# One queue of loads that the planner spaces by transfer time, layer norm of blocks 4 to 7 turned on TensorE, and all Q and K casts on ScalarE

## The chip, the cores and the metric

The kernel runs on 1 core of one Trainium2 chip. The metric is the device time of one execution in microseconds (us). A core has five instruction streams that run side by side and meet through semaphores: PE (TensorE, matmuls and their weight loads PEld), DVE (VectorE), ACT (ScalarE), POOL (GpSimd) and SP (SyncE), which here issues all DMAs but one. Each stream executes its instructions in program order, so an instruction that waits holds up everything behind it on its engine. This holds for SP as well.

## What is computed

A transformer block with modulation on x of 2048 tokens by 448 channels, in bfloat16. Cut to what matters:

```
sa, ca, ga, sb, cb, gb = split(silu(c) @ w_mod, 6)
h   = layernorm(x) * (1 + ca) + sa                       # LN1
q, k, v = split(h @ wqkv)                                # 16 heads of 28
o   = softmax over 8 keys at distances 0, 2, .. 14 (q k) v
x   = x + ga * (o @ wo)
h   = layernorm(x) * (1 + cb) + sb
y   = layernorm(h)                                       # LN of the MLP
x   = x + gb * (gelu(y @ w1 + b1) @ w2 + b2)             # hidden size 1792
```

## The kernel before

The tokens are 16 blocks of 128 (`NBLK`), even tokens in blocks 0 to 7 and odd ones in 8 to 15, so that the dilation of 2 becomes plain neighbourhood. The front of a block (`front_ln`, `front_qk`) is LN1 on token rows, a turn to channel rows (`hT`), and the products Q, K (`pq`) and V (`pv`). Blocks 0 and 1, then 2 and 3, then 4 to 7, 8 to 11 and 12 to 15 go together; we call the last three chunks 1, 2 and 3. V is written to memory (`v_hbm`, L712) and read back in windows (`vb`, L772), one pair of loads for each of nine attention steps b = 0 to 8 of 228 queries. An attention step is `lt` (logits, PE), Exp on ACT, a mask on DVE (`et`), `pd` and `po` on PE (denominator and output), Ln and Exp on ACT, and a product on DVE (`oT`). Then come `pw` (output projection), LN2 and the LN of the MLP on DVE, a DMA transpose to `yT` (L893), and for every 512 tokens the MLP: `p` at L578 and L584 (w1), gelu on ACT (L927), and `p` at L938 (w2).

How LN1 is turned is decided in `front_ln` by `early`. Chunk 0 (blocks 0 to 3) is turned on PE (`ptr`, L632), and ACT and DVE scale the result out of PSUM (L645, L641). The others are turned by DMA transposes on SP (L650, four for a chunk), after which DVE scales them in SBUF (L654). The row scale comes from two small ACT instructions for chunk 0 and from POOL for the others. `front_qk` lets eight casts of a chunk leave PSUM, and `QKE` says which by ACT (L694, A) and which by DVE (L691, D).

The order of every engine's work is made by a planner when the program is built (`Planner`): each piece of work is a task with an engine, a cost in us, and `late`, the time from its end until its result can be used. The planner plays the engines forward by priority and emits the tasks in the order in which it started them, so its costs set the order. For loads, `load` counts an issue of 0.5 us and keeps a running estimate of when the queue will be free; all its loads are chained by `order_after`, in the order in which they are written. `bulk` does the same for the MLP's weights, chained behind the load of `mod_bc` (the modulation rows for all partitions, L734).

Of the kernel before, what the change touches and what calls it, by code (L numbers as in the profile page):

```python
# [12 lines left out]
BF16 = mybir.dt.bfloat16  # L13
# [64 lines left out]
class Planner:  # L78
# [6 lines left out]
    def add(self, eng, us, fn, reads=(), writes=(), bufs=(), after=(), order_after=(), rank_add=0.0, late=0.0, dense=1.0, port=False, mode="F"):  # L85
        t = Task(len(self.tasks), eng, us, fn, bufs, rank_add, late, dense, port or eng == "POOL", mode)
# [191 lines left out]
def kernel(  # L278
# [14 lines left out]
    nc = tc.nc  # L293
# [6 lines left out]
    add = P.add  # L300
# [6 lines left out]
    def ps_one(shape, name, dtype=FP32):  # L307
        return Buf("S", lambda k: ps.tile(shape, dtype, name=name, tag=f"S{k}"), name)
# [18 lines left out]
    gbb2_bc = cst.tile([128, D], FP32, name="gbb2_bc")  # L327
    b1_bf = cst.tile([128, FT], BF16, name="b1_bf")
    b1_col = cst.tile([128, FT], FP32, name="b1_col")
# [36 lines left out]

    dma = {"free": 0.0, "at": 0.0, "last": []}

    def load(fn, nbytes, writes, reads=(), bufs=()):
        issue = 0.5  # L370
        dma["at"] += issue
        start = max(dma["free"], dma["at"] + 0.6)
        dma["free"] = start + nbytes / 360e3
        t = add("SP", issue, fn, writes=writes, reads=reads, bufs=bufs, late=dma["free"] + 1.0 - dma["at"],
                order_after=dma["last"])
        dma["last"] = [t]
        return t

    def load_k(dst, src, key, bufs=()):
        n = src.shape[1]  # L380
        for h in range(2):
            load(lambda h=h: nc.sync.dma_start(out=dst()[:, 2 * h:2 * h + 2],
                                               in_=src[KOFF[2 * h]:KOFF[2 * h] + 256].rearrange("(kt p) n -> p kt n", p=128)),
                 256 * n * 2, [key + "ab"[h]], bufs=bufs)

    def load_x(b0, b1):
        load(lambda: nc.sync.dma_start(out=x_all[:, b0:b1, :], in_=xv[b0 // 8, :, b0 % 8:(b1 - 1) % 8 + 1, :]),
             (b1 - b0) * 128 * D * 2, [f"x{b}" for b in range(b0, b1)])

    def bulk(fn, nbytes, writes, bufs=()):  # L390
        us = nbytes / 300e3
        t = add("SP", us, fn, writes=writes, bufs=bufs, late=2.5, order_after=dma["last"])
        dma["last"] = [t]

# [30 lines left out]
    def load_mlp():
        bulk(lambda: nc.sync.dma_start(out=b2_bc.t[:], in_=B_b2.partition_broadcast(128)), 128 * D * 2, ["b2"], [b2_bc])
        bulk(lambda: nc.sync.dma_start(out=b1_bf[:], in_=B_b1.rearrange("(f p) -> p f", p=128)), 150e3, ["b1_bf"])
        for kt in range(KT):
            bulk(lambda kt=kt: nc.sync.dma_start(out=w1_s[:, kt], in_=B_w1[KOFF[kt]:KOFF[kt] + 128]), F * 256, [f"w1{kt}"])
        for i in range(4):  # L430
            f0, f1 = 4 * i, min(4 * i + 4, FT)
            bulk(lambda f0=f0, f1=f1: nc.sync.dma_start(
                out=w2_s[:, f0:f1], in_=B_w2[128 * f0:128 * f1].rearrange("(ft p) n -> p ft n", p=128)),
                (f1 - f0) * 256 * D, [f"w2l{f // 2}" for f in range(f0, f1, 2)])
        add("DVE", 0.1, lambda: nc.vector.tensor_copy(out=b1_col[:], in_=b1_bf[:]), reads=["b1_bf"], writes=["b1"])

# [234 lines left out]
    def front_qk(bs, engs):  # L671
# [24 lines left out]
        for b in bs[::2]:  # L696
# [10 lines left out]
            for i in range(2):  # L707
# [9 lines left out]
    def mods():  # L717
# [3 lines left out]
        def mm():  # L721
# [243 lines left out]
    for pi, (blocks, tiles) in enumerate(PHASES):  # L965
        exps.clear()
        lt_mms.clear()
        for b in blocks:
            attention(b, tbl, prev_w1)
            if b in FRONTS:  # L970
                fc = FRONTS.index(b) + 1
                bs = list(range(4 * fc, 4 * fc + 4))
                front_ln(bs)
                front_qk(bs, QKE[1])
                if fc == 1:
                    mods()
                if fc == 2:
# [43 lines left out]
```

## Time and profile before

| | us |
|---|---|
| median of 3 runs | 188.71 (188.1 to 189.67) |
| the profiled execution | 188.94 |
| its span in the trace | 187.2 |
| busy in the span: PE, DVE, ACT, POOL | 166.3, 119.9, 103.4, 46.8 |

In the rows below, busy times are sums over an engine's instructions, "idle before" is the time that the engine stood before a group with what released it in brackets, and SPq rows are DMA issues (their length is the time until SP goes on, not that of the transfer). PEclk is the granted TensorE clock as a share of full speed: 1.00 is 2.4 GHz and 0.50 is 1.2 GHz. A matmul row's start is exact, its end is modelled.

### The profile page before, as it was taken

Reading aid. Unit: us, or ns where it says so; the run is one execution under the profiler, and the core shown is the slowest. Engines: PE = TensorE matmul, PEld = TensorE weight load, DVE = VectorE, ACT = ScalarE, POOL = GpSimd, SP = SyncE. Lnnn points to the kernel's source line nnn. Section 1 sums busy time; section 2 is a strip of 40 time slices with the busy share of each in tenths; the row PEclk is TensorE's granted clock in tenths of the full one; section 3 lists DMA queues with packets and bytes.
Section 4 is the critical chain, followed back from the end, with each engine's and each line's share of the span. In section 5 each row is a group of like instructions: output and inputs, shape, how many; then the busy total and the mean of one; then the engine's idle time right before and its main releaser. Section 6 shows DMA issues by size and latency. Waiting matters only on the chain.

```text
span 187.2 us, 4950 instructions
## 1 busy us (share of the span) xinstructions
PE 166.3 (89%) x2039; PEld 77.1 (41%) x2053; DVE 119.9 (64%) x329; ACT 103.4 (55%) x181; POOL 46.8 (25%) x81
## 2 busy tenths in 40 slices
PE   7799903699999799999999999999899999999992
PEld 2455402134444343433455434455433445333550
DVE  2798360894999999899844507998769982001121
ACT  3249626058548875947867883756863720365200
POOL 4062000150073433024422002458132353000000
PEclk9999965589999999999999999999999999999999
DMA  5999834499577893430151310005500025000011
GB/s 166 360 380 289 230 84 104 147 200 209 126 199 255 261 225 112 82 122 0 39 76 53 88 28 0 4 1 157 62 2 0 4 56 154 0 0 27 26 49 49
DMA packets 32649, 20.71 MB, mean 111 GB/s; under 512 B 18069, under 2 KB 31986, under 8 KB 32626
## 3 DMA queue, kind: packets, MB, share of 16 engines
q1 hardware_dynamic: 32624, 20.39, 41.0%
q8 instruction: 16, 0.26, 0.6%
q14 instruction: 7, 0.06, 0.1%
q10 hardware_dynamic: 2, 0.00, 0.0%
HBM read 12.75 MB, written 3.96 MB: 89 GB/s over the span
## 4 chain that ended last, share of the span: by engine, by line
PE 68%; DMA 16%; DVE 7%; SPq 3%; issue 2%; ACT 2%; DVEq 0%
PE p L938 21%; PE p L578 20%; PE pq L578 10%; DMA x_all<-in_A_x_dram 6%; PE p L584 4%; PE pw L867 4%; DMA yT<-y 3%; DMA wmod<-in_w_mod_dram 3%; DMA wqk_st<-in_A_wqkv_dram 3%; PE pv L578 3%; PE pq L584 2%; DVE st_all L501 2%; DVE et L804 2%; SPq L650 2%; PE po L826 1%
## 5 line engine op out<-in xcount | busy, mean ns | idle before, releaser
L927 ACT ACTIVATE hm<-p,b_col 128x512 bf16<-128x512 f32 x56 | 35.2, 686 | 29.2 <-PE p L584 13.4
L938 PE MATMUL p<-w_s,hm 128*128 128x448 bf16 x224 | 44.9, 353 | 0.0
L578 PE MATMUL p<-yT,w_s 128*128 128x512 bf16 x160 | 38.2, 380 | 2.1 <-DMA yT<-y 1.2
L519 POOL TENSOR_TENSOR rs_all<-tv_all,neg_half 128x1 f32<-128x1 f32 (+1 forms) x35 | 23.3, 677 | 56.4 <-DVE tv_all L516 51.5
L578 PE MATMUL pq<-hT,Wqk 128*128 128x512 bf16 (+1 forms) x115 | 25.3, 350 | 5.5 <-DVE hT L654 4.5
L938 PEld LDWEIGHTS <-hm 128*128 128x128 bf16 x224 | 20.9, 98 | 19.7 <-issue 0.9
L897 POOL TENSOR_TENSOR x1p<-x_all,gbb_bc 128x448 f32<-128x448 bf16 x16 | 17.0, 1072 | 46.2 <-DVE x_all L871 37.8
L945 DVE TENSOR_TENSOR x_all<-p,x1p 128x448 bf16<-128x448 f32 x16 | 9.8, 619 | 29.0 <-PE p L938 28.9
L796 ACT ACTIVATE et<-lt 128x464 bf16<-128x464 f32 x36 | 17.3, 565 | 13.9 <-PE lt L786 13.9
L578 PEld LDWEIGHTS <-w_s 128*128 128x128 bf16 x168 | 15.2, 98 | 22.7 <-issue 6.8
L501 DVE BATCH_NORM_STATS2 st_all<-x_all 128x6 f32<-128x448 bf16 x32 | 18.8, 611 | 3.8 <-DMA x_all<-in_A_x_dram 3.7
L578 PEld LDWEIGHTS <-Wqk 128*128 128x128 bf16 x120 | 10.5, 100 | 16.7 <-issue 5.8
L524 DVE TENSOR_SCALAR z<-x_all,mv,rs_all 128x512 bf16<-128x512 bf16 (+1 forms) x32 | 12.8, 417 | 3.9 <-DMA hT<-z 2.3
L871 DVE TENSOR_TENSOR x_all<-pw,x_all 128x448 bf16<-128x448 f32 x16 | 9.6, 618 | 8.2 <-PE pw L867 8.2
L804 DVE TENSOR_TENSOR et<-et,mask 128x928 bf16<-128x928 bf16 x18 | 12.5, 727 | 3.3 <-ACT et L796 3.3
L867 PE MATMUL pw<-wo_s,oT 128*128 128x448 bf16 x64 | 13.8, 354 | 0.7 <-DVE oT L852 0.7
L852 DVE TENSOR_TENSOR oT<-po,den 128x456 bf16<-128x456 f32 x18 | 10.6, 623 | 2.9 <-ACT den L842 2.9
L694 ACT CAST kT<-pq 128x512 bf16<-128x512 f32 (+1 forms) x15 | 7.3, 505 | 7.7 <-PE pq L584 5.6
L826 PE MATMUL po<-et,vb 64*32 64x57 bf16 x576 | 6.7, 195 | 5.2 <-DMA vb<-v_hbm 5.2
L708 ACT CAST vstage<-pv 128x448 bf16<-128x448 f32 x16 | 7.9, 540 | 5.2 <-PE pv L584 4.4
L578 PE MATMUL pv<-Wv,hT 128*128 128x448 bf16 x48 | 10.5, 354 | 0.0
L694 ACT CAST qT<-pq 128x512 bf16<-128x512 f32 (+1 forms) x15 | 7.1, 502 | 5.8 <-PE pq L584 3.7
(81 smaller groups left out, 169.5 us busy)
## 6 DMA issues: line engine op xcount, KB each, us to landing
w_s<-in_B_w_dram SPq DMA_DIRECT2D x7, 448.0 KB
vb<-v_hbm SPq DMA_DIRECT2D x18, 128.0 KB, 2.7
v_hbm<-vstage SPq DMA_DIRECT2D x8, 256.0 KB, 2.6
wmod<-in_w_mod_dram SPq DMA_DIRECT2D x4, 448.0 KB, 7.2
out_dram<-x_all SPq DMA_DIRECT2D x8, 224.0 KB, 2.3
wqk_st<-in_A_wqkv_dram SPq DMA_DIRECT2D x4, 226.0 KB, 5.2
wm_st<-in_w_mod_dram SPq DMA_DIRECT2D x2, 448.0 KB
x_all<-in_A_x_dram SPq DMA_DIRECT2D x1, 896.0 KB, 10.4
```

What stands on the lines that cost most here:

```text
L501: add("DVE", 0.53, lambda: nc.vector.bn_stats(out=st_all[:, sl, :], in_=src()), reads=key, writes=[f"st{sl}"])
L519: lambda: nc.gpsimd.tensor_tensor(out=rs_all[:, which, b0:b0 + n], in0=tv_all[:, which, b0:b0 + n], in1=neg_half[:, 0:n], op=ALU.pow),
L524: return add("DVE", us, lambda: nc.vector.tensor_scalar(out=dst(), in0=src(), scalar1=mv[:, b, 0:1], scalar2=rs_all[:, which, b:b + 1], op ...
L578: nc.tensor.matmul(outs[i].t[:], lhsT=w(i, kt, slice(0, 128)), rhs=x(i, kt, slice(0, 128)), start=(n == 0 and not last), stop=(n == 2 and ...
L584: nc.tensor.matmul(outs[i].t[:], lhsT=w(i, kt, rows), rhs=x(i, kt, rows), start=not last, stop=last, tile_position=(r0, 0))
L694: add("ACT", 0.06 + n / 1200, lambda dst=dst, p=pq[i]: nc.scalar.copy(out=dst, in_=p.t[:]), bufs=[pq[i]], writes=w)
L796: ex = add("ACT", 0.45, lambda r=r: nc.scalar.activation(out=et.t[:, r].rearrange("p n ft c -> p (n ft c)"), in_=lts[r].t[:].rearrange("p ...
L804: nc.vector.tensor_tensor(out=ev, in0=ev, in1=mask[:], op=ALU.mult)
L867: nc.tensor.matmul(pw.t[:], lhsT=oT[:, ft, c0:c0 + 128], rhs=wo_s[:, ft, :], start=(ft == 0), stop=(ft == 3))
L897: P.wrote(add("POOL", 1.05, lambda: nc.gpsimd.tensor_tensor(out=xp.t[:], in0=x_all[:, t, :], in1=gbb2_bc[:], op=ALU.add), reads=[f"x{t}", ...
L927: gl = add("ACT", 0.57, lambda f=f, p=p1[i]: nc.scalar.activation(out=hm_at(f), in_=p.t[:], func=ACT.Gelu_apprx_tanh, bias=b1_col[:, f:f + ...
L938: nc.tensor.matmul(p2.t[:], lhsT=hm_at(f)[:, bi * 128:(bi + 1) * 128], rhs=w2_s[:, f, :], start=(f == 0), stop=(f == FT - 1))
```

## The change

It does six things. Every load gets a planner cost of its bytes divided by `DMA_RATE` (330 GB/s, at least 0.5 us) on SP and a `late` of 1.8. Only the first loads, to x of blocks 4 to 7, stay chained; the others are `free` and the planner places each where its priority puts it. The load of x of blocks 8 to 15 becomes two of 448 KB. Chunk 1 becomes `early`. All Q and K casts go to ACT. And b1 arrives as 14 rows and is turned by one small matmul (`b1_cols`).

```diff
-QKE = ("ADAAADAA", "ADAAADAA")
+QKE = ("AAAAAAAA", "AAAAAAAA")
...
+DMA_RATE = 330e3
...
-    def load(fn, nbytes, writes, reads=(), bufs=()):
-        issue = 0.5
-        dma["at"] += issue
-        start = max(dma["free"], dma["at"] + 0.6)
-        dma["free"] = start + nbytes / 360e3
-        t = add("SP", issue, fn, writes=writes, reads=reads, bufs=bufs, late=dma["free"] + 1.0 - dma["at"],
-                order_after=dma["last"])
-        dma["last"] = [t]
-        return t
+    chain_dma = []
+
+    def load(fn, nbytes, writes, reads=(), bufs=(), free=False):
+        t = add("SP", max(0.5, nbytes / DMA_RATE), fn, writes=writes, reads=reads, bufs=bufs, late=1.8,
+                order_after=list(chain_dma))
+        if not free:
+            chain_dma[:] = [t]
...
-    load_x(8, 16)
+    for b in (8, 12):
+        load_x(b, b + 4)
...
-        early = ch == 0
+        early = ch <= 1
...
-            add("SP", 0.5, lambda r0=r0, vs=vs: nc.sync.dma_start(
+            add("SP", 0.8, lambda r0=r0, vs=vs: nc.sync.dma_start(
                 out=v_hbm[r0:r0 + 256].rearrange("(b p) n -> p b n", p=128), in_=vs.t[:].rearrange("p b h d -> p b (h d)")),
...
-        add("SP", 0.5, lambda: nc.sync.dma_start(out=mod_bc[:], in_=mod_hbm[:].rearrange("i n -> (i n)").partition_broadcast(128)),
+        add("SP", 1.4, lambda: nc.sync.dma_start(out=mod_bc[:], in_=mod_hbm[:].rearrange("i n -> (i n)").partition_broadcast(128)),
             reads=["mod_hbm"], writes=["ga", "sb", "g2", "gb"], late=3.2)
-        dma["last"] = [P.tasks[-1]]
-        load_mlp()
...
+    def b1_cols():
+        pb1 = ps_one([128, FT], "pb1")
+        P.wrote(add("PE", 0.1, lambda: nc.tensor.matmul(pb1.t[:], lhsT=b1_rows[:], rhs=ident[0:FT, 0:FT], start=True, stop=True),
+                    mode="32x128", reads=["b1_rows", "ident"], bufs=[pb1]), pb1)
+        add("DVE", 0.1, lambda: nc.vector.tensor_copy(out=b1_col[:], in_=pb1.t[:]), bufs=[pb1], writes=["b1"])
```

The MLP's loads, before in `load_mlp`, stand behind the two loads of x as `free` loads; the wmod loads (`w_mod`, for the later modulation rows), the four of wo and `v_pads` are `free` too.

The first place is SP, before, from the loads of the later modulation weights (two tiles, two halves each) to the DMA transposes of chunk 1. wo is the output projection, `vstage_105` and `vstage_106` hold V of two blocks each.

```order
L382 DMA wmod_214<-in_w_mod_dram 128x2x896 x2
L420 DMA wo_s<-in_A_wo_dram 28x4x448 x4
L387 DMA x_all<-in_A_x_dram 128x8x448
L712 DMA v_hbm<-vstage_105 128x2x512
L772 DMA vb<-v_hbm 64x2x512 x2
L650 DMA_TRANSPOSE hT<-z 128x4x128 x4
L712 DMA v_hbm<-vstage_106 128x2x512
L732 DMA mod_hbm<-mod_rows 4x448
```

The same place with the change. The line numbers are those of the changed file: 379, 384 and 412 are the loads, 702 and 766 the V store and the `vb` load, 722 and 724 the modulation rows, 640 the DMA transposes, which here are those of chunk 2.

```order
L379 DMA wmod_253<-in_w_mod_dram 128x2x896
L702 DMA v_hbm<-vstage_105 128x2x512
L384 DMA x_all<-in_A_x_dram 128x4x448
L412 DMA wo_s<-in_A_wo_dram 28x4x448 x2
L766 DMA vb<-v_hbm 64x2x512 x2
L384 DMA x_all<-in_A_x_dram 128x4x448
L722 DMA mod_hbm<-mod_rows 4x448
L412 DMA wo_s<-in_A_wo_dram 28x4x448
L702 DMA v_hbm<-vstage_106 128x2x512
L412 DMA wo_s<-in_A_wo_dram 28x4x448
L420 DMA w_s<-in_B_w_dram 128x1792
L724 DMA mod_bc<-mod_hbm 128x1792
L640 DMA_TRANSPOSE hT<-z 128x4x128 x4
```

The V store of blocks 0 and 1 moved ahead of wo and of x of blocks 8 to 15, and the `vb` pair that waits for it ahead of x of 12 to 15. No transpose stands between them any more, and the transposes of chunk 2 stand behind `mod_bc` and a w1 piece.

The second place is DVE from the scaling of blocks 2 and 3 on, before.

```order
L641 TENSOR_SCALAR hT<-ptr,mod_col 128x256 x2
L524 TENSOR_SCALAR z<-x_all,mv_100,rs_all 128x512 x4
L804 TENSOR_TENSOR et<-et,mask 128x928 x2
L691 CAST kT<-pq 128x256
L691 CAST qT<-pq 128x256
L501 BN_STATS st_all<-x_all 128x6 x3
```

And with the change, where 631 is the scaling out of PSUM, 514 the normalization, 798 the mask and 491 the statistics.

```order
L631 TENSOR_SCALAR hT<-ptr,mod_col 128x256 x2
L514 TENSOR_SCALAR z<-x_all,mv_100,rs_all 128x512 x4
L798 TENSOR_TENSOR et<-et,mask 128x928 x2
L631 TENSOR_SCALAR hT<-ptr,mod_col 128x512 x2
L491 BN_STATS st_all<-x_all 128x6 x2
```

The two casts are gone and the scaling of chunk 1 stands in their place, ahead of the statistics of blocks 8 to 11. Before, chunk 1 was scaled behind those statistics.

On PE, between the modulation rows (`pb`) and `pd` of attention step 0 there was nothing before. With the change two pairs of `pq` of blocks 2 and 3, `pv` of blocks 4 and 5 and one pair of `pq` of chunk 1 stand there, and the sixteen PE transposes of chunk 1 stand just ahead of `pb`.

The third place is SP with the change, ahead of the first MLP tile: 887 is the transpose to `yT` (four of these make the first tile) and the vb load stands between the third and the fourth.

```order
L887 DMA_TRANSPOSE yT<-y 128x4x128
L766 DMA vb<-v_hbm 64x2x512 x3
L887 DMA_TRANSPOSE yT<-y 128x4x128
L766 DMA vb<-v_hbm 64x2x512
L887 DMA_TRANSPOSE yT<-y 128x4x128
L702 DMA v_hbm<-vstage_106 128x2x512
```

Before, the second to fourth of these four transposes stood together, ahead of a pair of `vb` loads.

## Rows read from the trace of the kernel before

**Rows 1.** Windows by stage: busy us of each engine, clock, DMA share, GB/s.

```profile
core 0: us, PE busy (x) PEld busy (x) DVE busy (x) ACT busy (x) POOL busy (x), PEclk, DMA share, GB/s
0.00:22.70 22.70, 19.85 (x232) 10.70 (x235) 14.44 (x49) 11.79 (x30) 6.46 (x30) 1.00 0.95 293
22.70:34.30 11.60, 1.85 (x144) 1.39 (x140) 4.46 (x14) 4.38 (x8) 0.00 (x0) 0.60 0.39 96
34.30:48.50 14.20, 13.91 (x186) 5.48 (x188) 10.57 (x28) 7.53 (x13) 3.23 (x3) 0.84 0.86 190
48.50:80.50 32.00, 29.30 (x470) 13.21 (x473) 30.83 (x83) 23.36 (x42) 10.43 (x14) 1.00 0.65 176
80.50:187.20 106.70, 101.37 (x1016) 46.36 (x1024) 59.64 (x160) 56.30 (x88) 26.71 (x34) 1.00 0.18 43
28.30:38.60 10.30, 5.53 (x139) 2.42 (x141) 4.96 (x16) 3.44 (x6) 1.02 (x1) 0.50 0.54 143
```

**Rows 2.** Timeline of PE around its two longest waits: start, us, operation.

```profile
28.32 0.73 PE L826 MATMUL po<-et,vb 64*32 64x57 bf16 x64 [5.23 <-DMA vb<-v_hbm]
...
34.31 0.61 PE L578 MATMUL pq<-hT,Wqk 128*128 128x512 bf16 x1 [4.53 <-DVE hT L654]
```

**Rows 3.** Timeline of SP's DMA issues in the same stretch.

```profile
7.85 2.31 SPq L382 DMA_DIRECT2D wmod<-in_w_mod_dram  x4
...
13.62 0.39 SPq L387 DMA_DIRECT2D x_all<-in_A_x_dram  x1
14.88 2.03 SPq L712 DMA_DIRECT2D v_hbm<-vstage  x1
24.75 1.33 SPq L772 DMA_DIRECT2D vb<-v_hbm  x2
26.17 5.22 SPq L650 DMA_TRANSPOSE hT<-z  x4
```

**Rows 4.** Pieces of the chain of work that ended last: start, us, what.

```profile
13.62 10.44 DMA x_all<-in_A_x_dram
...
30.18 2.44 DMA hT<-z
```

**Rows 5.** DMA issues of the page: KB each, us to landing.

```profile
vb<-v_hbm SPq DMA_DIRECT2D x18, 128.0 KB, 2.7
v_hbm<-vstage SPq DMA_DIRECT2D x8, 256.0 KB, 2.6
wmod<-in_w_mod_dram SPq DMA_DIRECT2D x4, 448.0 KB, 7.2
```

**Rows 6.** Timeline of DVE: normalization of chunk 1, its scaling.

```profile
16.70 1.37 DVE L524 TENSOR_SCALAR z<-x_all,mv,rs_all 128x512 bf16<-128x512 bf16 x4
...
32.74 1.52 DVE L654 TENSOR_SCALAR hT<-hT,mod_col 128x512 bf16<-128x512 bf16 x4 [5.72 <-DMA hT<-z]
```

**Rows 7.** Timeline of PE: the transposes of chunk 0.

```profile
7.33 0.61 PE L632 MATMUL ptr<-ident,z 128*128 128x128 bf16 x8
...
15.12 0.90 PE L632 MATMUL ptr<-ident,z 128*128 128x128 bf16 x8
```

**Rows 8.** By line: durations in ns, least, median and most.

```profile
L691 DVE CAST qT<-pq x5: 392/681/692, 11.0 to 72.8; 128x512 bf16<-128x512 f32 x3, 128x256 bf16<-128x256 f32 x2
L694 ACT CAST qT<-pq x15: 372/586/592, 10.7 to 75.4; 128x512 bf16<-128x512 f32 x9, 128x256 bf16<-128x256 f32 x6
L645 ACT ACTIVATE hT<-ptr,mod_col x4: 553/561/566, 8.5 to 16.3; 128x256 bf16<-128x256 bf16 x4
L632 PE MATMUL ptr<-ident,z x16: 216/219/230, 7.3 to 15.8; 128*128 128x128 bf16 x16
```

**Rows 9.** Timeline of PE where the first MLP tile begins.

```profile
77.60 1.31 PE L578 MATMUL pv<-Wv,hT 128*128 128x448 bf16 x6
79.24 0.93 PE L867 MATMUL pw<-wo_s,oT 128*128 128x448 bf16 x4 [0.33 <-DVE oT L852]
80.51 1.46 PE L578 MATMUL p<-yT,w_s 128*128 128x512 bf16 x5 [0.34 <-DMA yT<-y]
```

More of the change, by code (lines that the diff above doesn't have):

```diff
@@ L85, in add @@
     def add(self, eng, us, fn, reads=(), writes=(), bufs=(), after=(), order_after=(), rank_add=0.0, late=0.0, dense=1.0, port=False, mode="F"):
-        t = Task(len(self.tasks), eng, us, fn, bufs, rank_add, late, dense, port or eng == "POOL", mode)
+        t = Task(len(self.tasks), eng, us, fn, bufs, rank_add, late, dense, (port or eng == "POOL") and port is not None, mode)
         for k in list(reads) + [b for b in bufs]:
@@ L327 @@
     gbb2_bc = cst.tile([128, D], FP32, name="gbb2_bc")
-    b1_bf = cst.tile([128, FT], BF16, name="b1_bf")
+    b1_rows = cst.tile([FT, 128], BF16, name="b1_rows")
     b1_col = cst.tile([128, FT], FP32, name="b1_col")
@@ L365, in wide, with load_k @@
         return bass.AP(ap.tensor, ap.offset, [ap.ap[0], [KOFF[2], 2], [1, 256]])
-    dma = {"free": 0.0, "at": 0.0, "last": []}
-    def load(fn, nbytes, writes, reads=(), bufs=()):
-        issue = 0.5
-        dma["at"] += issue
-        start = max(dma["free"], dma["at"] + 0.6)
-        dma["free"] = start + nbytes / 360e3
-        t = add("SP", issue, fn, writes=writes, reads=reads, bufs=bufs, late=dma["free"] + 1.0 - dma["at"],
-                order_after=dma["last"])
-        dma["last"] = [t]
-        return t
-    def load_k(dst, src, key, bufs=()):
+    chain_dma = []
[4 more added lines that the diff above has]
+            chain_dma[:] = [t]
+    def load_k(dst, src, key, bufs=(), free=False):
         n = src.shape[1]
@@ L383, in load_k @@
                                                in_=src[KOFF[2 * h]:KOFF[2 * h] + 256].rearrange("(kt p) n -> p kt n", p=128)),
-                 256 * n * 2, [key + "ab"[h]], bufs=bufs)
+                 256 * n * 2, [key + "ab"[h]], bufs=bufs, free=free)
     def load_x(b0, b1):
         load(lambda: nc.sync.dma_start(out=x_all[:, b0:b1, :], in_=xv[b0 // 8, :, b0 % 8:(b1 - 1) % 8 + 1, :]),
[L388 to L393, printed above, removed]
+             (b1 - b0) * 128 * D * 2, [f"x{b}" for b in range(b0, b1)], free=b0 >= 8)
     add("DVE", 0.2, lambda: nc.vector.memset(warm_w[:], 0.0), writes=["warm_w"], rank_add=500)
@@ L412, in v_pads @@
                           in_=z.unsqueeze(1).to_broadcast([LEAD, 3, DP]))
-    load(v_pads, 3 * LEAD * DP * 2, ["v_pads"], reads=["warm_w"])
+    load(v_pads, 3 * LEAD * DP * 2, ["v_pads"], reads=["warm_w"], free=True)
     for i in range(2):
-        load_k(lambda i=i: wmod2[i].t[:], w_mod[:, (2 + 2 * i) * D:(4 + 2 * i) * D], f"wmod2{i}", [wmod2[i]])
+        load_k(lambda i=i: wmod2[i].t[:], w_mod[:, (2 + 2 * i) * D:(4 + 2 * i) * D], f"wmod2{i}", [wmod2[i]], free=True)
     add("POOL", 1.6, lambda: nc.gpsimd.memset(wo_s[:], 0.0), writes=["wo"], rank_add=440)
@@ L420 @@
         load(lambda r=r: nc.sync.dma_start(out=wo_s[HP * r:HP * r + DH, :, :], in_=wo_v[r]), D * D // 2, [f"wo{r}"],
-             reads=["wo"])
-    load_x(8, 16)
+             reads=["wo"], free=True)
+    for b in (8, 12):
+        load_x(b, b + 4)
     b2_bc = sb("zh", [128, D], BF16, "b2_bc")
[L425 to L435, printed above, removed]
+    load(lambda: nc.sync.dma_start(out=b2_bc.t[:], in_=B_b2.partition_broadcast(128)), 128 * D * 2, ["b2"], bufs=[b2_bc], free=True)
+    load(lambda: nc.sync.dma_start(out=b1_rows[:], in_=B_b1.rearrange("(f p) -> f p", p=128)), F * 2, ["b1_rows"], free=True)
+    for kt in range(KT):
+        load(lambda kt=kt: nc.sync.dma_start(out=w1_s[:, kt], in_=B_w1[KOFF[kt]:KOFF[kt] + 128]), F * 256, [f"w1{kt}"], free=True)
+    for i in range(4):
+        f0, f1 = 4 * i, min(4 * i + 4, FT)
+        load(lambda f0=f0, f1=f1: nc.sync.dma_start(
+            out=w2_s[:, f0:f1], in_=B_w2[128 * f0:128 * f1].rearrange("(ft p) n -> p ft n", p=128)),
+            (f1 - f0) * 256 * D, [f"w2l{f // 2}" for f in range(f0, f1, 2)], free=True)
     def pool(us, fn, writes, reads=(), rank_add=300, gated=True):
@@ L976 @@
                     mods()
+                    b1_cols()
                 if fc == 2:
```

## The prediction

> **What bounds the kernel now.** I began with the busy time by stage [rows 1]. From 80.5 us to the end PE is busy for 101.37 of 106.70 us at full clock. The change puts no new instruction there, so I let that stretch pass unchanged: a start that is earlier by some amount ends earlier by the same amount. From 48.5 to 80.5 PE is busy for 29.30 of 32.00 us and DVE for 30.83, so DVE is nearly full and PE stands still for 2.70. The odd stretch is 22.70 to 34.30: PE is busy for 1.85 of 11.60, and neither DVE (4.46) nor ACT (4.38) fills it. Nothing computes, so something is on its way.
>
> The timeline of PE names two waits [rows 2]: 5.23 us for the `vb` load of attention step 0 and 4.53 us for the scaled `hT` of chunk 1. The clock adds to them: after PE has stood still, the rows from 28.30 to 38.60 show a granted clock of 0.50 (1.2 GHz), with 5.53 us of PE busy in them [rows 1].
>
> Why both come late is seen on SP [rows 3, 4]. The load of x of blocks 8 to 15, 896 KB, is issued at 13.62 and has landed 10.44 later, at 24.06. The V store of blocks 0 and 1 is issued at 14.88, behind it on the same queue. The `vb` pair must wait for that store and is issued at 24.75. The four transposes of chunk 1 stand behind the pair: they begin at 26.17 and take SP 5.22 us, the last lands 2.44 after 30.18, and DVE scales for 1.52 more. Yet the token rows of chunk 1 were normalized by 16.70 + 1.37 = 18.07 [rows 6].
>
> **LN1 of chunk 1 on PE.** It takes four DMA transposes off SP. Instead PE gets sixteen. The trace has eight in 0.61 and eight in 0.90 us [rows 7], so sixteen cost 1.2 to 1.8; I take 1.5, since the second row has a gap that may come again. Each is 219 ns long when looked at alone [rows 8], so 3.5 would be the price if none overlapped. The b1 matmul is smaller than one of them; I give it 0.1. The Trainium skill speaks against this step: TensorE: Matmul & The Clock Gate, "Part 4: PE-mode transpose", gives about 275 ns for a 128x128 transpose inside a kernel; an estimate by that figure is 4.4 us for sixteen, and the time would be 2.9 later than mine. This trace does not agree, since eight of them began and ended within 0.61 us.
>
> Scaling out of PSUM: DVE has two instructions of 512 columns, which I price as its cast of 512 out of PSUM, 0.69 at most, so 1.4 against the 1.52 that go [rows 6, 8]: nothing. ACT has two new ones of 512. At 256 one takes 561 ns [rows 8], so a lies between 0.56 and 1.12; an ACT cast grows from 372 to 586 from 256 to 512, so I take 0.8, 1.6 for both, off the path unless ACT fills.
>
> When is chunk 1 ready? Its rows end at 18.07 now. Its row scale moves to ACT, behind the scaling of blocks 2 and 3, and costs about 1.5, so 19.6. PE turns it until 21.1, DVE and ACT scale it until about 22.5 to 23. Now it is ready at 34.26. PE meanwhile has `pb` and two pairs of blocks 2 and 3 to do, so it finds chunk 1 ready. Its one wait is for the normalized rows ahead of the transposes: 0 to 1.5, I take 0.6.
>
> **The order of the loads.** With the change only the wmod loads stand ahead of the V store: the last is issued at about 9.8, and with the median of 7.2 us to landing [rows 3, 5] it is in at 17. The store is issued about 15.3 (its casts stand behind two more ACT casts), and lands 2.6 later when alone: 17.9 at the earliest, 2.6 after wmod, 19.6, if it queues behind it, and 24.75 at the latest, as now; I take 19.5. The `vb` pair takes SP 1.33, and 644 KB of x and wo are ahead of it on the queue, 2.2 us at the 293 GB/s of the first stage [rows 1]. That puts `vb` at about 24 instead of 28.32. PE comes to it at about 27.5, because two pairs, one `pv` and one pair of chunk 1 stand ahead of it now. So this wait goes, and with `vb` at the old time it would be 0.8.
>
> So 9.75 us of standing still (11.60 - 1.85) have work to put in. If PE does not stand still the half clock goes too: 5.53 us of work at half speed are 2.77 at full speed, another 2.77.
>
> **The casts.** Ten leave DVE, six of 512 and four of 256: 6 x 0.68 + 4 x 0.40 = 5.7 us. ACT gains 6 x 0.586 + 4 x 0.37 = 5.0 [rows 8]. Four of the large ones lie between 48.5 and 80.5. DVE falls there from 30.83 to about 28.1, ACT rises from 23.36 to 25.7 of 32 [rows 1]. What it gives is at least nothing and at most the 2.70 that PE stands still there. I take 1.3, the middle, since part of PE's idle time is a wait for ACT or for a DMA, which a lighter DVE does not shorten. But earlier, from about 24 to 41, ACT has casts of two chunks, two attention steps and V to do, about 17 us of work by the rows' durations, so it is full. Stalls of PE for PSUM that ACT has not emptied cost 0 to 3; I take 1.2.
>
> **The first MLP tile.** On SP the third and fourth transposes to `yT` now have `vb` loads ahead of them and between them, of which the last need the buffers that `po` of steps 3 and 4 free. After the last `po` come 0.6 for the load's issue, two transposes of 1.3 (5.22 for four) and 2.44 to land [rows 3, 4], about 5.6 us. PE has a `pv` (1.6) and three `pw` (0.8 each) to do [rows 9], about 4.0. The wait is then 1.6, where now 0.33 and 0.34 are waited for: 0.9 lost, between -0.7 and 2.
>
> The rest is hidden: more DMA issues on SP stand where SP waits, b1 and b2 are issued well ahead of the MLP and of the first use of b2, and the halves of x carry the same bytes.
>
> **The sum.** Gained: 9.75 + 2.77 + 1.3 = 13.8. Lost: 1.6 + 0.6 + 1.2 + 0.9 = 4.3. That is 9.5 us off the profiled execution's own 188.94, so **179.4 us**. The median of the three runs is 188.71, 0.2 below it, which I leave in the range. With every term at its good end (13.8 + 1.4, less 1.3, and the `yT` wait gone) the gain is 14.6, time 174.3; with the bad ends (transposes 3.5, waits 1.5 + 3 + 2, nothing from the casts) it is 2.4, time 186.5.
>
> **Rivals.**
> *Chunk 2 becomes the new wait.* PE now begins chunk 2 at about 48.5 and would come there at about 39. Its chain is long: x of 12 to 15 is loaded behind the `vb` pair, its statistics stand ahead of the normalization of chunk 2 on DVE, and its four transposes stand on SP behind `mod_bc` and a w1 piece. By my count x of 12 to 15 is issued at 21.2, behind the `vb` pair, and lands at 25 behind 900 KB at 293 GB/s; its statistics end at 27, four normalizations (1.37) at 28.5; four transposes take SP from 27.5 to 33 (5.22) and land at 35.7 (2.44); DVE has two masks of step 1 ahead of the scaling (1.52) and ends at 38.4. There is no slack. If the 896 KB of `mod_bc` and w1 hold the queue (3.1 us at 293 GB/s) and DVE comes later by 2, PE stands for 5 us: 184.4. For it: these waits are of the kind that is removed. Against it: the queue is empty of x and wmod by then.
> *ACT becomes the bound of both stages.* Then PE stalls for 3 us early, and the casts give nothing later: 179.4 + 1.8 + 1.3 = 182.5. Against it: 25.7 of 32 is not full.
> *No change.* The waits are refilled one for one because PE has to reach `yT` at a time that DVE sets. DVE is busy for 46 of the 58 us after 22.7 [rows 1], so it would have to stand still as much as now: 188.5.
> *Slower.* One chain on SP does it: `mod_bc` waits for the rows of `pb` to be stored, and all transposes of chunk 2 stand behind it. If they come so late that PE stands longer than the 9.5 us won, that is if chunk 2 is ready only after 48.9, the half clock that follows is lost again too: 188.94 + 2.77 = 191.7. Against it: PE does `pb` at about 22 in both, and the store behind it had to wait for SP until 32 only because SP was held.
>
> **Chances.** My sum 0.62 (its own range 176.5 to 182), late chunk 2 0.17, ACT 0.11, no change 0.05, slower 0.05. The range takes in the first three: 175 to 185. A measurement of this kernel can tell about 1% from no change, so: faster 0.89, same 0.06, slower 0.05.
>
> **What would show it.** The profile after should have: sixteen transposes near 20 us in under 2 us; the V store landed by 21 and no PE wait for `vb` over 1 us; granted clock 1.00 from 22 to 40; chunk 2's first product at 38 to 40; DVE under 90% in the last stage ahead of the MLP; the first MLP tile at about 71 instead of 80.51 [rows 9]; the stretch behind it within 1.5 us of 106.7. I am wrong if PE waits for `hT` of chunk 2 for more than 3 us, if the clock falls again, or if the MLP stretch changes.

## The result, and the profile after

The changed kernel takes 181.05 us (median of 4 runs, 179.47 to 182.87) against 189.19 of the kernel before beside it: a ratio of 0.954 with a 95% interval of 0.944 to 0.964. One hundredth of the ratio is 1.9 us. All ratios here leave out executions more than 1.5% above the fastest of the same kernel, and the medians do not, so a ratio need not be that of two medians. The changed kernel's profiled execution took 179.47 us, with a span of 177.8 (before: 188.94 and 187.2).

First the windows by stage; the first answers to the second window of [rows 1]. The other three are cut at marks that both kernels have: the `pv` of blocks 2 and 3, the first product of chunk 2, and the first MLP product.

```profile
core 0: us, PE busy (x) PEld busy (x) DVE busy (x) ACT busy (x) POOL busy (x), PEclk, DMA share, GB/s
22.70:34.30 11.60, 11.25 (x193) 5.23 (x192) 8.47 (x26) 9.47 (x21) 2.05 (x2) 1.00 1.04 202
16.93:37.26 20.33, 19.98 (x329) 10.34 (x330) 16.17 (x45) 16.68 (x38) 2.05 (x2) 1.00 0.92 203
37.26:71.70 34.44, 30.69 (x547) 14.02 (x547) 29.11 (x74) 27.22 (x50) 11.07 (x14) 1.00 0.73 188
71.70:177.80 106.10, 102.30 (x1024) 46.33 (x1024) 60.25 (x161) 56.10 (x88) 28.82 (x36) 0.99 0.16 41
```

The stretch from 22.70 to 34.30, in which PE was busy for 1.85 us, is full: 11.25 of 11.60, at full clock. The timeline of PE shows what stands there, and which waits are left further on (start, us, operation, idle time before it and its releaser).

```profile
19.33 1.07 PE L622 MATMUL ptr<-ident,z 128*128 128x128 bf16 x16
...
26.52 0.73 PE L820 MATMUL po<-et,vb 64*32 64x57 bf16 x64
...
37.26 0.39 PE L574 MATMUL pq<-hT,Wqk 64*128 64x512 bf16 x2
...
46.97 0.64 PE L820 MATMUL po<-et,vb 64*32 64x57 bf16 x60 [1.94 <-DVE oT L846]
...
70.59 0.93 PE L861 MATMUL pw<-wo_s,oT 128*128 128x448 bf16 x4 [1.23 <-DVE oT L846]
71.70 1.46 PE L568 MATMUL p<-yT,w_s 128*128 128x512 bf16 x6 [0.18 <-issue]
```

Both waits of [rows 2] are gone: `po` of step 0 begins at 26.52 and waits for nothing. Chunk 2 begins at 37.26. The first MLP product is at 71.70 instead of 80.51 [rows 9]. A new wait of 1.94 stands in step 2, and one of 1.23 ahead of the MLP (the `pw` at 70.59). On SP, where [rows 3] had the V store at 14.88 behind the 896 KB, the store now goes at 15.46 and the `vb` pair at 19.16:

```profile
15.46 0.37 SPq L702 DMA_DIRECT2D v_hbm<-vstage  x1
...
19.16 1.33 SPq L766 DMA_DIRECT2D vb<-v_hbm  x2
...
27.34 5.70 SPq L640 DMA_TRANSPOSE hT<-z  x4
```

### The profile page after: what moved, and what is told of

It is laid out like the page before. It is cut to its first block, busy times and chain, and to the rows that moved or that the text cites. A ratio compares the mean times of both kernels' runs of the same rounds, so it can differ in the third digit from the quotient of the medians.

```text
span 177.8 us, 4992 instructions
## 1 busy us (share of the span) xinstructions
PE 167.2 (94%) x2071; PEld 78.4 (44%) x2071; DVE 116.0 (65%) x316; ACT 107.8 (61%) x195; POOL 47.4 (27%) x80
## 4 chain that ended last, share of the span: by engine, by line
PE 73%; DMA 12%; DVE 6%; SPq 2%; ACT 2%; issue 1%; DVEq 0%
PE p L932 25%; PE p L568 21%; PE pw L861 6%; PE pq L568 5%; DMA hT<-z 5%; PE p L574 5%; DMA wm_st<-in_w_mod_dram 3%; PE pv L568 3%; PE lt L780 2%; DMA x_all<-in_A_x_dram 2%; DMA v_hbm<-vstage 2%; PE po L820 2%; DVE oT L846 2%; DVE st_all L491 1%; SPq L766 1%
## 5 line engine op out<-in xcount | busy, mean ns | idle before, releaser
L568 PE MATMUL p<-yT,w_s 128*128 128x512 bf16 x168 | 39.5, 380 | 0.2 <-issue 0.2
L568 PE MATMUL pq<-hT,Wqk 128*128 128x512 bf16 (+1 forms) x120 | 24.2, 338 | 0.2 <-issue 0.2
L798 DVE TENSOR_TENSOR et<-et,mask 128x928 bf16<-128x928 bf16 x18 | 11.6, 665 | 4.7 <-ACT et L790 4.6
L514 DVE TENSOR_SCALAR z<-x_all,mv,rs_all 128x512 bf16<-128x512 bf16 (+1 forms) x32 | 12.0, 395 | 3.5 <-ACT rs_all L500 2.0
L684 ACT CAST kT<-pq 128x512 bf16<-128x512 f32 (+1 forms) x20 | 9.4, 517 | 4.1 <-PE pq L574 3.3
L833 ACT ACTIVATE den<-pd 128x464 f32<-128x464 f32 x18 | 9.1, 566 | 3.5 <-PE pd L812 3.5
L684 ACT CAST qT<-pq 128x512 bf16<-128x512 f32 (+1 forms) x20 | 9.2, 509 | 1.3 <-PE pq L574 1.0
```

Source lines behind the costliest of these rows:

```text
L514: return add("DVE", us, lambda: nc.vector.tensor_scalar(out=dst(), in0=src(), scalar1=mv[:, b, 0:1], scalar2=rs_all[:, which, b:b + 1], op ...
L568: nc.tensor.matmul(outs[i].t[:], lhsT=w(i, kt, slice(0, 128)), rhs=x(i, kt, slice(0, 128)), start=(n == 0 and not last), stop=(n == 2 and ...
L684: add("ACT", 0.06 + n / 1200, lambda dst=dst, p=pq[i]: nc.scalar.copy(out=dst, in_=p.t[:]), bufs=[pq[i]], writes=w)
L798: nc.vector.tensor_tensor(out=ev, in0=ev, in1=mask[:], op=ALU.mult)
```

## The experiments

There are two kinds. In the first the changed kernel keeps its planned order, and one thing is undone or moved in it; `move(a, b)` puts the tasks `a` ahead of the first task `b` in the finished plan, on whatever engine they run. In the second kind one part of the change is made or left out, and the planner makes a new order.

### Order kept

**Chunk 1 by DMA transposes.** At the place of the first PE transposes of chunk 1 its four DMA transposes are issued; all four scalings are done by DVE.

```diff
+                    if ch == 1:
+                        for b in bs if half == 0 else ():
+                            nc.sync.dma_start_transpose(out=hc.t[:, :, b % 4 * 128:b % 4 * 128 + 128], in_=zs[b].t[:])
+                        return
```

> The changed kernel with its planned order kept, and only chunk 1 turned by four DMA transposes again (issued on SP where the PE transposes stood, all four scaled by DVE). Theory (the turn on PE is the main part of the gain): the transposes take SP from about 18.7 to 24 us, the last lands at 26.4, chunk 1 is scaled at about 28, PE stands still for about 5 us in front of it, and vb and x of blocks 12 to 15 are held back by the same 5 us: 5 to 7 us slower than the changed kernel, 186 to 188 us. Rival (the new order of the loads alone removes the wait): within 1.5 us of the changed kernel, 180 to 182.5.

Measured: 185.61 us median, ratio 0.969 (0.961 to 0.977). PE in this kernel has three waits that the changed kernel does not have or has shorter: 0.90 us for chunk 2's rows at 41.38, and these two.

```profile
24.93 1.95 PE L568 MATMUL pv<-Wv,hT 128*128 128x448 bf16 x6 [3.33 <-DVE hT L635]
...
53.22 0.67 PE L826 MATMUL po<-et,vb 64*32 64x57 bf16 x60 [3.75 <-DVE oT L852]
```

Undoing this part gives back some 1.5 of the 4.6%, 2.9 us, less than expected: in this order the transposes stand at 17.56 on SP, earlier than the kernel before could issue them (26.17 in [rows 3]), and chunk 1 is ready at about 25.5, not at 34.26. The profiled execution took 187.26 us, with a granted clock of 0.50 from 26 to 29 and again from 54 to 56, and the other three took 182.70, 183.96 and 191.69. The stages of the profiled execution, below, overstate the loss.

**The old place of the loads.** The loads of x of blocks 8 to 15 and of `wo` stand ahead of the first V store again.

```diff
     P.plan()
+    move(lambda t: t in loads, lambda t: t is v_stores[0])
     P.emit()
```

> The changed kernel with its planned order kept, and only the loads of x of blocks 8 to 15 and of wo moved ahead of the first V store on SP, as before the change. Theory (my sum: chunk 1 on PE gives PE work until 26.3 us, so only the rest of the vb wait comes back): vb lands at about 28, PE waits about 2 us for it, 182 to 184 us. Rival 1 (load order is the main part): 5 us or more slower than the changed kernel, 186 and more. Rival 2 (the order of the loads is worth nothing once chunk 1 is on PE): within 1 us, 180 to 182.

Measured: 182.47 us, ratio 0.963 (0.956 to 0.970), so about 0.9% or 1.7 us above the changed kernel, though the intervals overlap. The trace shows where. SP and PE in this kernel:

```profile
16.41 0.39 SPq L705 DMA_DIRECT2D v_hbm<-vstage  x1
24.26 1.33 SPq L770 DMA_DIRECT2D vb<-v_hbm  x2
```

```profile
27.56 0.68 PE L824 MATMUL po<-et,vb 64*32 64x57 bf16 x64 [1.12 <-DMA vb<-v_hbm]
```

From the store's issue it takes 7.85 us until the pair can go (24.26 - 16.41) instead of 3.70 (19.16 - 15.46), and PE waits 1.12 for `vb`. The prediction had 0.8 for this. The late V rows cost 5.23 before because PE had nothing else; with chunk 1 ready ahead of them most of that wait is covered. The expected 2 us of waiting was too much, the expected time of 182 to 184 held.

**Ten casts back on DVE.** Of the eight casts of a chunk two are DVE's again, each at its place in the order.

```diff
-    nc.scalar.copy(out=dst, in_=p.t[:])
+    (nc.vector.tensor_copy if m in (1, 5) else nc.scalar.copy)(out=dst, in_=p.t[:])
```

> The changed kernel with its planned order kept, and only the ten casts of Q and K that were on DVE before put back on DVE, at the place in its order where ACT did them. Theory (casts are worth 1.3 us, at most 2.7, less what ACT loses): 0 to 1.5 us slower, 181 to 182.5. Rival (relief of DVE, full at 96% before, is a main part): 3 us or more slower, 184 and more. Second rival (ACT is the tighter engine early on): faster than the changed kernel.

Measured: 183.26 us, ratio 0.969 (0.965 to 0.974). By the times alone the casts on ACT seem worth 2 to 3 us: all four executions, 183.04 to 183.81, lie above every execution of the changed kernel. The one trace says otherwise, see the table below.

**Chunk 3's transposes ahead of the `vb` pair.** On DVE the scalings of chunk 3 wait for DMA transposes, and `oT` of step 1, for which PE waits 1.94, stands behind them:

```profile
44.86 0.41 DVE L644 TENSOR_SCALAR hT<-hT,mod_col 128x512 bf16<-128x512 bf16 x1 [2.94 <-DMA hT<-z]
...
46.29 1.17 DVE L846 TENSOR_TENSOR oT<-po,den 128x456 bf16<-128x456 f32 x2
```

The last two of these transposes stand on SP behind the `vb` pair of step 2. Here they go first.

```diff
     P.plan()
+    move(lambda t: t in turned[4:], lambda t: t is vb_loads[4])
     P.emit()
```

> The changed kernel with one move: on SP the last two DMA transposes of chunk 3 go ahead of the vb pair of attention step 2. In the changed kernel po of step 2 waits 1.94 us for oT of step 1, which on DVE stands behind the scaling of chunk 3, which waits 2.94 us for these transposes. Theory (that vb pair on SP is the cause): chunk 3 lands about 2.2 us earlier, the wait goes, 1 to 2 us faster, 179 to 180. Rival (the wait comes from ACT's Exp of step 1 or is taken up by later waits ahead of the MLP): within 0.5 us of the changed kernel.

Measured: 181.19 us, ratio 0.958 (0.954 to 0.962), no gain. The wait of 1.94 became one of 1.05 for the `vb` that now comes later and one of 1.01 for `oT`:

```profile
46.26 0.21 PE L823 MATMUL po<-et,vb 64*32 64x57 bf16 x4 [1.05 <-DMA vb<-v_hbm]
47.47 0.70 PE L823 MATMUL po<-et,vb 64*32 64x57 bf16 x60 [1.01 <-DVE oT L849]
```

**`oT` of step 1 ahead of chunk 3's scalings.** The same wait, taken away on DVE.

```diff
     P.plan()
+    move(lambda t: t in divs[2:4], lambda t: t in scales[4:])
     P.emit()
```

> The changed kernel in its planned order, with one move on DVE: the two normalizations of attention's output of step 1 (oT) stand ahead of the four scalings of chunk 3, not behind them. Their inputs are there by about 43.5, while DVE stands idle for 2.9 us before the scalings. Theory A (the 1.94 us that PE waits for oT in step 2 is a loss that this order makes, and it reaches the end): PE does not wait there, the first MLP product comes 1.5 to 2 us earlier, and the time is 1 to 1.9 below the changed kernel's run beside it. Theory B (the wait only moves on, to chunk 3's rows or to the next V rows, as it did when the transposes were moved): within 0.5 of the changed kernel, with another wait of 1 us or more before the MLP.

In this kernel the moved `oT` also passed ACT's Exp of step 1's denominators in the order of the program. It multiplies by their logarithm instead, Exp comes after it, and `oT` runs some 1.8 us sooner than it could with the right input (at 41.76; in the changed kernel Exp ends at 43.51). An estimate from these rows: begun at 43.51 and 1.17 long, it would still end at 44.68, ahead of chunk 3's scalings, which begin at 44.73 here. The amount of work is the same, but the output is not the block's. Measured: 179.62 us, ratio 0.952 (0.946 to 0.959), not distinguishable from the changed kernel. Its PE does not wait in step 2, and yet the MLP begins at 71.41, only 0.29 sooner, because these two waits are there instead:

```profile
65.62 0.35 PE L574 MATMUL pv<-Wv,hT 64*128 64x448 bf16 x1 [1.93 <-DVE oT L848]
...
70.64 0.93 PE L864 MATMUL pw<-wo_s,oT 128*128 128x448 bf16 x4 [1.92 <-DVE oT L848]
```

Its POOL and DVE show the reason of the first, which lies elsewhere:

```profile
63.05 1.03 POOL L733 TENSOR_TENSOR gbb_bc<-mod_bc,b_bc 128x448 f32<-128x448 bf16 x1 [6.00 <-DMA b_bc<-in_B_b_dram]
```

```profile
64.61 0.41 DVE L514 TENSOR_SCALAR y<-h,mv,rs_all 128x512 bf16<-128x512 bf16 x1 [2.96 <-POOL rs_all L509]
64.94 1.17 DVE L848 TENSOR_TENSOR oT<-po,den 128x456 bf16<-128x456 f32 x2
```

POOL waits 6.00 us for the load of b2, three row scales (`rs_all`) stand behind it on POOL, the normalization to `y` waits 2.96 for them on DVE, and `oT` stands behind `y`. Then PE waits. The `oT` of the second wait comes at 69.42, behind two scalings of w2 that take DVE 2.84 us (66.66). The changed kernel has the same load at the same place (issued at 55.43, POOL released at 61.95), and POOL waits 2.77 for it:

```profile
61.95 1.52 POOL L731 TENSOR_TENSOR gbb_bc<-mod_bc,b_bc 128x448 f32<-128x448 bf16 x1 [2.77 <-DMA b_bc<-in_B_b_dram]
```

So the wait in step 2 could be taken away and almost nothing came of it (0.29 us at the MLP), since the next ones were already due. An earlier issue of the b2 load was not tried.

**The changed kernel once more.**

> The changed kernel once more, unaltered, beside the run above. Every theory expects its ratio to the kernel before within the interval measured first, 0.944 to 0.964; how far its own profile's stages move from the first profile's says what a difference between two single profiles can mean.

Measured: 181.66 us median (178.4 to 182.16), 0.958 of the 189.56 of the kernel before beside it. The profiled execution took 181.34 us, 1.87 more than the first one, from the same program. The stage from chunk 2 to the MLP took 2.46 us longer, the one ahead of it 0.53 less. In step 2 PE waited 2.38 us instead of 1.94, and then the granted clock fell (windows of this execution):

```profile
44.00:47.90 3.90, 1.52 (x76) 0.94 (x76) 2.91 (x9) 3.05 (x5) 0.65 (x1) 1.00 0.91 282
47.90:51.60 3.70, 3.70 (x12) 1.09 (x11) 2.49 (x5) 0.00 (x0) 0.00 (x0) 0.54 0.85 267
```

PE was busy for 1.52 of 3.90 us, and the 3.70 behind that ran at 0.54, near the lower level of 1.2 GHz: 3.70 x (1 - 0.54) = 1.7 us lost, with the longer wait 2.1 of the 2.46.

With this the stages of the kernels that keep the order can be set side by side. The first stage begins at the `pv` of blocks 2 and 3 and ends at chunk 2's first product, the second ends at the first MLP product; the starts are read from each kernel's timeline of PE.

| kernel | start | first stage | second stage | half clock in the second | MLP to the end |
|---|---|---|---|---|---|
| changed | 16.93 | 20.33 | 34.44 | no | 106.10 |
| the same again | 16.88 | 19.80 | 36.90 | 47.9 to 51.6 | 106.02 |
| chunk 1 by DMA | 16.41 | 24.97 | 38.09 | 53 to 56.6 | 106.13 |
| old loads | 16.66 | 21.92 | 34.36 | no | 106.06 |
| casts on DVE | 18.87 | 19.81 | 36.94 | 50.4 to 53.9 | 106.08 |
| chunk 3's transposes first | 16.86 | 20.32 | 36.56 | 47.3 to 50.7 | 106.16 |
| `oT` first | 16.77 | 19.81 | 34.83 | no | 106.09 |

The casts on DVE have the stages of the second look at the changed kernel to within 0.06 us. What is 2 us longer is the start, and that has to do with the clock as well:

```profile
7.68 0.90 PE L548 MATMUL ps_col<-silu_bf,wm_st 128*128 128x1 bf16 x30 [1.35 <-DMA wm_st<-in_w_mod_dram]
```

```profile
8.50:12.10 3.60, 3.55 (x22) 1.85 (x20) 3.23 (x11) 1.02 (x2) 0.89 (x11) 0.63 1.09 369
```

PE waited 1.35 us for the first weights (0.96 in the changed kernel's profile), and the granted clock from 8.50 to 12.10 was 0.63. All of the start's 1.94 us are there at the second group of `pq` (12.77 against 10.83 in the changed kernel), and the first cast comes only at 13.10. So in this execution the ten casts cost nothing that its stages show, and what it took longer than the changed kernel's first profile goes with the clock and the waits ahead of its falls. What the casts cost stays open all the same, for two reasons. They may have had a part in the longer wait in step 2 (2.59), behind which the clock was 0.52 from 50.40 to 53.90. And of the three executions without a kept trace two, 183.04 and 183.12 us, have a mean granted clock of 0.990 and 0.991 on record, as the changed kernel has it in executions of 180.6 to 182.16; the clock does not account for them.

### Planned anew

**One part alone.** First the kernel before with chunk 1 on PE:

```diff
-        early = ch == 0
+        early = ch <= 1
```

> The kernel before with one edit: blocks 4 to 7 are also transposed on PE (early = ch <= 1), and the planner plans anew. Loads and the casts of Q and K are as before, so the V rows of step 0 still land behind the bulk loads. In its plan PE's first product with vb stands behind nearly all products of chunk 1, not ahead of them. Theory A (the wait that cost most was that for chunk 1's normalized rows, and the late vb is then covered by other work): about 181, 95 to 97 per cent of the kernel before. Theory B (both waits must go together, because PE still stops at vb): 185 to 187, PE waits 3 us or more for vb. Theory C (the transposes on PE are worth nothing alone): 188 to 189.

Then the changed kernel with chunk 1 and the casts as before, so that the new loads remain:

```diff
-QKE = ("AAAAAAAA", "AAAAAAAA")
+QKE = ("ADAAADAA", "ADAAADAA")
...
-        early = ch <= 1
+        early = ch == 0
```

> The changed kernel with its loads, but blocks 4 to 7 transposed by DMA as before and the casts of Q and K as before, planned anew. Theory A (the transposes on PE carry the larger part): 184 to 186; PE does not wait for vb, but some 3 to 5 us for the normalized rows of chunk 1. Theory B (the loads carry nearly all): 180 to 182. Theory C (the loads alone are worth nothing): 188 or more.

And the kernel before with all casts on ACT:

```diff
-QKE = ("ADAAADAA", "ADAAADAA")
+QKE = ("AAAAAAAA", "AAAAAAAA")
```

> The kernel before with all casts of Q and K on ACT, planned anew; nothing else. The prediction's term: 1.3 us gained on the way to the last stage (0 to 2.7) less 1.2 where ACT empties PSUM later (0 to 3), so 188 to 189. Theory A (in this kernel too the two cancel): within 1 per cent of the kernel before. Theory B (the casts delay DVE's normalization of attention's output, and are a gain of their own, as putting them back in the changed kernel cost 2 us): 186 to 187. Theory C (ACT becomes the engine that is waited for): 190 to 192.

Measured, as ratios to the kernel before: chunk 1 on PE 0.973 (0.966 to 0.980), the loads 0.982 (0.974 to 0.990), the casts 0.998 (0.993 to 1.003). Chunk 1 on PE alone (185.23 us median) has the time of Theory B without its wait: PE does not stop for `vb`, since `po` of step 0 stands behind most of chunk 1 there. But the first product of chunk 2 comes at 43.48, and PE waits 1.01 us at 36.61 for a cast on DVE and twice for `oT`, the longer here and 0.80 at 53.79:

```profile
41.30 0.78 PE L786 MATMUL lt<-qT,kT 28*64 28x58 bf16 x63 [1.99 <-DVE oT L852]
```

With the loads alone (186.78 us, above Theory A's 184 to 186) PE waits 1.37 us for `vb` and 0.96 for chunk 1's rows, where [rows 2] had 5.23 and 4.53, but at half clock for much of it:

```profile
28.20 0.71 PE L820 MATMUL po<-et,vb 64*32 64x57 bf16 x64 [1.37 <-DMA vb<-v_hbm]
29.87 0.61 PE L574 MATMUL pq<-hT,Wqk 64*128 64x512 bf16 x2 [0.96 <-DVE hT L644]
30.41 5.12 PE L568 MATMUL pq<-hT,Wqk 128*128 128x512 bf16 x12
```

The twelve `pq` of 512 columns take 5.12 us there; at full clock six take 1.47. The casts alone (189.45 us) leave the wait for `vb` as it was (5.62 us), and the time too.

**Two parts, and other seeds.** The changed kernel with the casts split as before:

```diff
-QKE = ("AAAAAAAA", "AAAAAAAA")
+QKE = ("ADAAADAA", "ADAAADAA")
```

> The changed kernel with the casts of Q and K split between ACT and DVE as before, but planned anew (the run with the casts put back kept the changed kernel's order). Theory A (the casts on ACT are worth about nothing once the planner can place them): within 1 per cent of the changed kernel, 179.5 to 182.5. Theory B (they are worth the prediction's net of 0.1 or up to 2 us, since DVE is fullest in the last stage): 182.5 to 184. Theory C (ACT alone is too slow, so the split is better): 178 to 179.5.

And the changed kernel, then the kernel before, with another seed of the planner's search:

```diff
-SEED, TURNS = 44, 60
+SEED, TURNS = 45, 60
```

> The changed kernel with the planner's random seed 45 for 44: the same operations and loads, another order found by the search. It prices the plan itself. Theory A (the gain belongs to the three edits, not to one lucky order): 179 to 183, within 1 per cent of the changed kernel. Theory B (a good part belongs to the order that seed 44 found): 184 to 187.

> The kernel before with the planner's random seed 45 for 44, nothing else. Theory A (its two stops, for vb and for chunk 1's rows, come from the loads and the DMA transposes and not from one order): 187 to 190.5 with PE stopped 8 us or more for the two together between 21 and 36 us. Theory B (the stops belong to the order that seed 44 found): 183 to 186.

Measured: without the casts 0.995 (0.990 to 0.999), 188.18 us, slower than any theory had it; the changed kernel with the other seed 0.943 (0.935 to 0.950); the kernel before with it 1.015 (1.002 to 1.029), also slower than expected. A new order of the same operations is worth 1 to 1.5% either way, and so no single number of this kind is the price of its part. The clock blurs it further: in the traces of all kernels planned anew but chunk 1 alone it was 0.50 to 0.63 from 9.00 to 12.00, where it was 1.00 in the kernel before and the changed one. The kernel with the casts split as before shows how a gain gets lost. It enters chunk 2 at 38.75, 1.49 later than the changed kernel, and has by then not done one pair of `pv` and the logits of step 2, which take the changed kernel 2.23 (35.03 to 37.26): 3.7 of its lead is gone. The first of these waits is in that part, the others come behind it:

```profile
37.16 0.93 PE L861 MATMUL pw<-wo_s,oT 128*128 128x448 bf16 x4 [2.62 <-DVE oT L846]
...
69.67 0.71 PE L780 MATMUL lt<-qT,kT 28*64 28x58 bf16 x61 [2.59 <-DVE x_all L865]
...
77.42 1.46 PE L568 MATMUL p<-yT,w_s 128*128 128x512 bf16 x6 [1.39 <-DMA yT<-y]
```

From chunk 2 to the MLP it takes 38.67 us (77.42 - 38.75) against 34.44, but with those 2.23 of work in it, so 2.0 are lost there. The clock has a part in both losses: it was 0.50 from 9.50 to 11.00, and 0.54 from 70.40 to 73.70, behind the wait of 2.59. DVE is busy for 34.03 of the 38.67. How the loss divides between the casts on DVE, the order and the clock is not shown. In the kernel before with the other seed the two stops are there again (2.92 and 0.74 us for `vb`, 4.87 for chunk 1's rows), as Theory A had it: they come from the loads and the DMA transposes, not from one order.

## Why the prediction was right, and where its steps were not

The forecast was 179.4 us, in a range of 175 to 185, made against the profiled execution: 188.94 less 9.5. The profiled execution after is 179.47, 9.47 less. The median, 181.05, is 1.6 above that; two profiles of this kernel differ by as much (1.87), most of it through the clock in step 2. That the total is right to 0.1 is luck: 1.3 more than forecast up to chunk 2, 2.0 less from there to the MLP and 0.6 behind it that was not counted cancel out. The mechanism, two stops filled with work and no half clock behind them, is what the traces show.

**Up to chunk 2 more was gained than forecast.** The kernel before stands at the same point at 48.51, at the end of the logits of step 2:

```profile
44.32 0.39 PE L818 MATMUL pd<-et,ones_k 64*32 64x464 bf16 x8
44.53 0.73 PE L826 MATMUL po<-et,vb 64*32 64x57 bf16 x64
...
47.77 0.74 PE L786 MATMUL lt<-qT,kT 28*64 28x58 bf16 x64
```

By then it had also done `pd` and `po` of step 1 (44.32 to 45.19, 0.87), which the changed kernel does later. So the lead is 48.51 - 37.26 - 0.87 = 10.38 us. The forecast's terms for this part were 9.75 + 2.77 - 1.6 - 0.6 - 1.2 = 9.1. The two gains held: PE busy for 11.25 of 11.60, clock 1.00. The losses were smaller than their prices:
- Sixteen PE transposes took 1.07 us, not 1.5. The rule that the forecast weighed against them (the Trainium skill, TensorE: Matmul & The Clock Gate, "Part 4: PE-mode transpose", about 275 ns each) is not what this trace shows for a row of them: one by itself lasts 219 ns [rows 8], sixteen together 67 ns each (1.07 / 16).
- PE did not wait for the normalized rows (0.6 forecast): they end at 19.01 and the transposes begin at 19.33.
- For PSUM that ACT had not emptied PE shows no wait of its own ahead of chunk 2, and one of 0.18 at 66.07, not 1.2. Its one wait for ACT in that part is 0.35 at 16.93, for scaled rows of chunk 0.
- Chunk 1 was ready at 21.44, by DVE and ACT both, not at 22.5 to 23.
- The V store had landed by 19.16 (forecast 19.5), and `vb` was there when PE came to it at 26.52.

**Chunk 2 was as tight as the rival said, and in time.** The chain was forecast to end at 38.4. DVE waited for x of blocks 12 to 15 until 24.79 (forecast 25), had normalized chunk 2 at 28.35 (28.5), SP turned it from 27.34 to 33.04 (27.5 to 33), and DVE ended the scaling at 37.15 (35.78 + 1.37). PE came at 37.26, 0.11 later. No wait, and no slack. This is the end of the chain on DVE, four scalings:

```profile
35.78 1.37 DVE L644 TENSOR_SCALAR hT<-hT,mod_col 128x512 bf16<-128x512 bf16 x4
```

**From chunk 2 to the MLP the forecast failed.** It had 1.3 gained by the casts and 0.9 lost to `yT`, 0.4 in all. The kernel before takes 80.51 - 48.51 + 0.87 = 32.87 us for the same work and the changed kernel 34.44: 1.57 lost. The step that failed is that a lighter DVE gives PE some of its idle time back. Before, 2.1 of PE's 2.70 idle here were waits for DVE, 0.70 for `oT` and 1.42 for a mask, so the term had a ground:

```profile
65.60 0.39 PE L818 MATMUL pd<-et,ones_k 64*32 64x464 bf16 x8 [1.42 <-DVE et L804]
```

DVE did get lighter, busy for 29.11 of 34.44 (85%, forecast under 90), and this wait is gone, but two others for `oT` came in its place. The 1.94 comes while DVE itself stands still for 2.94, for the DMA transposes of chunk 3; DVE is not short of time there. The 1.23 comes from what stands ahead of `oT` in the order: its denominators are there at 68.51 (the end of Exp on ACT), and DVE is at two scalings of w2.

```profile
67.45 2.00 DVE L742 TENSOR_TENSOR w_s<-w_s,mod_bc 128x896 bf16<-128x896 bf16 x2
69.37 1.16 DVE L846 TENSOR_TENSOR oT<-po,den 128x456 bf16<-128x456 f32 x2
```

So the 1.3 of the casts do not show in the sum of this part; what the casts are worth by themselves the runs leave open, as said above. The wait for `yT` of 1.6 did not come; PE had 0.18 there, since it came later itself.

**"The rest is hidden" was wrong for b2.** The load of b2 was said to be issued well ahead of its use. It is one of the loads that are free in the change, is issued at 55.43, and POOL waits 2.77 for it, with row scales behind it on POOL. In the changed kernel DVE waits 0.15 for these and PE hardly feels that; with the wait of step 2 gone it did.

**The MLP stretch** took 106.10 against 106.70, within the bound of 1.5, and gave 0.6 that was not counted. All kernels that keep the order have 106.0 to 106.2, so it goes with the order; why is not settled. Of the signs that the forecast named, chunk 2's first product came ahead of its 38 to 40, and one spoke against it in the second look at the kernel: the clock fell again, behind the wait in step 2. The balance of the spans: 10.38 - 1.57 + 0.59 = 9.40, which is 187.2 - 177.8.

Which of the three parts carried it? With the order kept, chunk 1 back on DMA gives back 1.5% and the old loads 0.9%; the casts 1.5% by the times, and nothing by the one trace. Neither undoing gives back the 4.6%. The traces suggest why: each of the first two parts covers the wait that the other leaves. Chunk 1, when it is ready, is work ahead of `vb` (1.12 of waiting with the old loads, where the kernel before has 5.23), and an early `vb` lets `po` and what follows go ahead of the rest of chunk 1. Both undone at once with the order kept was not run, so that the two together carry the whole is argued and not shown. Alone and planned anew they gave 2.7 and 1.8%, in sum near the whole, which that reading does not lead one to expect. How the gain divides between them more exactly than that can't be told, since an order that is planned anew differs by as much.

## What to carry to other kernels

When two waits stand one behind the other, look at what work each would uncover for the other: a chunk that is ready covers a late load. Price a part with the order of everything else kept, since a planner's new order moves the time by as much as the part. And of two profiles of one program read the clock first, for behind a wait that is 0.44 us longer the lower clock cost 1.7 here.

## What the runs showed of the hardware

The two kept traces of the changed kernel, 1.87 us apart, differ mostly by the granted clock behind one wait of PE. In step 2 it stayed at 1.00 behind a wait of 1.94 us, and was 0.54 for 3.70 us behind one of 2.38, which cost some 1.7 us. That is not the whole spread: of this kernel's eight executions those of 182.87 and 181.99 us have a mean granted clock of 1.000 on record, and those of 178.40 and 179.47 one of 0.996; why the former are longer is open.

The wait for the first weights shows the same over all fourteen traces. In the eight where it was 0.37 to 1.23 us the clock stayed at 1.00 from 9.00 to 12.00; in the six where it was 1.30 to 1.98 it was 0.50 to 0.63 there. In the trace with the casts on DVE that cost some 1.3 us (3.60 x 0.37). The kernels that keep the order are alike up to there and yet have 0.37 to 1.35, so the length of this wait belongs to the execution. Elsewhere length alone does not decide it: in the kernel planned anew with the casts split as before PE waited 2.62 us at 37.16 and the clock stayed at 1.00, and behind its wait of 2.59 at 69.67 it fell.

That waiting in between matmuls brings the lower clock is also what the Trainium skill says (TensorE: Matmul & The Clock Gate, "HAM oscillation — how this bites in real kernels"); the waits in its example are longer than these.
